# Transposing the logits' operand outside TensorE for 8 of 12 chunks of a fused attention and two-MoE kernel

## The chip, the cores and the metric

The kernel runs on one NeuronCore of a Trainium2 chip. The metric is the device time of one execution in microseconds (us), the median of several runs. Engines: PE is TensorE (PEld its weight loads), DVE is VectorE, ACT is ScalarE, POOL is GpSimd, SP is SyncE, whose queue issues every DMA of this kernel.

## The reference, cut to what matters

Block-causal attention is followed by a two-layer MLP and by a soft mixture of experts. Only the last one is touched: its `logits` need the tokens `x` with the model dimension on the partitions.

```python
# q, k, v: (8 batches, 8 heads, 576, 64), attention masked in blocks of 64
x = attn_out.transpose(0, 2, 1, 3).reshape(4608, 512)
h = np.maximum(x @ w_in, 0.0)             # 512 x 2048
x = h * h @ w_out                         # 2048 x 512
...
logits = x @ phi                          # 4608 x 512 by 512 x 32
d = np.exp(logits - logits.max(0)); d /= d.sum(0)
slot_input = d.T @ x                      # 32 slots x 512
slot_out = experts(slot_input)            # 8 experts, 4 slots each
c = np.exp(logits - logits.max(1)); c /= c.sum(1)
return c @ slot_out
```

## The kernel before, in words

The tokens are worked through in 12 chunks of 384 (three tiles of 128). A chunk of the MLP is 16 slots, one for each 128 columns of `w_in`. A slot has two parts on PE. `slot_h` (L808) makes 12 matmuls of 384 columns into the PSUM bank HB: the hidden layer of the slot, in three products, since weights and activations are each split in a high and a low part. ACT and DVE then make relu, square and the split (L814 to L819, tile MG). `slot_o` (L833) makes 9 matmuls of 512 columns into the three PSUM banks O, one for each token tile. The high parts of the weights (W) stay in SBUF; the low parts (WL) come back from DRAM for each slot, 512 KB, into one of three buffers (L800). A WL buffer is free when the sixth matmul of `slot_o`, three slots back, has read it, and it is needed by the second matmul of the slot's `slot_h`.

When a chunk's 16 slots are done, ACT (or DVE) copies the three O banks to X2 (L846, L847), and `moe2` does the soft mixture's part of the chunk beside the first slots of the next one. Before the change: 12 transposes on PE with the identity (L873), three copies from PSUM to the tile YA (L881, L882), the logits as 12 small matmuls that read YA (L888; each is two passes in the profile), a running maximum and sum, two more transposes (L917), and three matmuls of X2 (L940) that add to the slots' inputs. The attention of later batches (L447 scores, L456 to L493 softmax on DVE and ACT, L501 values) is spread over the slots too; it works in the SBUF tile aF and loads its keys and values through L433 and L434.

The order of the instructions on each engine is fixed when the program is built. `Program.order` plays the program through with costs per operation and gives each engine the ready operation of the earliest due time, so an operation that is expected later moves to a later place in the row, and the engine waits there if what it needs comes later still. Each engine works its row strictly in that order. SP too: a DMA that waits for data holds up every DMA behind it.

Of the kernel before, what the change touches and what calls it, by code (L numbers as in the profile page):

```python
# [7 lines left out]
F32 = mybir.dt.float32  # L8
# [7 lines left out]
NTOK, DM, DFF = B * S, H * D, 2048  # L16
NSLOT, NE, SPE, DFE = 32, 8, 4, 1024
KT = DM // 128
FT = DFF // 128
CH = 384  # L20
NCH = NTOK // CH
NTT = CH // 128
# [232 lines left out]
def c_tr(n):  # L255
    return 100 + 1.08 * n
# [6 lines left out]
def emit(tc, qk, v, vd, kq2, v2, w, phi, w1, w2, jsel, gsel, out):  # L263
    nc = tc.nc
    pe, act, dve, pool, sp = nc.tensor, nc.scalar, nc.vector, nc.gpsimd, nc.sync
    pr = Program()
# [8 lines left out]
    dram = tc.alloc_tile_pool(name="dram", bufs=1, space=bass.MemoryType.DRAM)  # L275
# [4 lines left out]
    BANKS = {"w": [psum.tile([128, 512], F32, name=f"B{t}") for t in range(4)], "w1": OB + [HB]}  # L280

    wlo_d = dram.tile([FT, 128, 1024], F32, name="wlo_d")
    part_d = dram.tile([NTT, 128, DM], F32, name="part_d")

    def bank(g):
        return BANKS[g.pool][g.bank]
# [5 lines left out]
    ph = cp.tile([128, KT, NSLOT], F32, name="ph")  # L292
# [4 lines left out]
    X2 = [cp.tile([128, DM], F32, name=f"X2_{i}") for i in range(NTT)]  # L297
    YA = cp.tile([128, NTT * DM], F32, name="YA")
# [20 lines left out]
    NPT = 2048  # L319
# [3 lines left out]
    L0, L1 = Lane(), Lane()  # L323
# [55 lines left out]
    def idle(keys):  # L379


        return [x for k in keys for x in list(pr.readers.get(k, ())) + ([pr.last_w[k]] if k in pr.last_w else [])]

    def parts(i):
        return range(2) if i == 4 else range(1)
# [4 lines left out]
    PT9, PH_ = 256, 2336  # L390
# [335 lines left out]
    YAK = [("YA", t) for t in range(NTT)]  # L726
# [132 lines left out]
    def moe2(c, m, due):  # L859

        z = m % 2
# [5 lines left out]
            return (nm, (z + o) % 2)  # L867

        xT = YA.rearrange("p (k n) -> p k n", k=KT)
        for t in range(NTT):  # L870
            g = Group("w")
            for k in range(KT):
                pr.add(("pe", c_mm(128), lambda g=g, t=t, k=k: pe.transpose(  # L873
                    bank(g)[:, k * 128:(k + 1) * 128], X2[t][:, k * 128:(k + 1) * 128], ident)),
                    r=[("X2", t), "id"], grp=g, take=(k == 0), due=due)
            d_ = xT[:, :, t * 128:(t + 1) * 128]

            def tb(g):
                return bank(g).rearrange("p (a b) -> p a b", a=KT)

            pr.add([("act", c_act(512), lambda g=g, d_=d_: act.copy(d_, tb(g))),  # L881
                    ("dve", c_tt(512), lambda g=g, d_=d_: dve.tensor_copy(d_, tb(g)))],  # L882
                   w=[("YA", t)], grp=g, give=True, due=due)
        g = Group("w")
        for k in range(KT):
            def mm(k=k, g=g):
                for t in range(NTT):
                    pe.matmul(bank(g)[32 * t:32 * t + 32, 0:128], ph[:, k], xT[:, k, t * 128:(t + 1) * 128],  # L888
                              start=(k == 0), stop=(k == KT - 1))
            pr.add(("pe", 206, mm), r=YAK + ["ph"], grp=g, take=(k == 0), due=due, mode=1)  # L890
        M, nM, sE = T("M"), T("nM"), T("sE")
        lg = g
        if m == 0:
            pr.add(("dve", c_tt(128), lambda: dve.reduce_max(M, bank(lg)[0:96, 0:128], axis=AX.X)),
                   w=[k2("M")], grp=g, due=due)
        else:
            mc = T("mc")
            pr.add(("dve", c_tt(128), lambda: dve.reduce_max(mc, bank(lg)[0:96, 0:128], axis=AX.X)),
                   w=[k2("mc")], grp=g, due=due)
# [8 lines left out]
        else:  # L908
            al = T("al")
            pr.add(("act", 188, lambda: act.activation(al, T("M", 1), AF.Exp, bias=nM)), r=[k2("M", 1), k2("nM")],  # L910
                   w=[k2("al")], due=due)
            pr.add(("dve", 70, lambda: dve.scalar_tensor_tensor(T("s"), T("s", 1), al, sE, ALU.mult, ALU.add)),
                   r=[k2("s", 1), k2("al"), k2("sE")], w=[k2("s")], due=due)
        g = Group("w")
# [123 lines left out]
    lR = [("a", nm, h) for h in range(2) for nm in ("hk", "hq", "ql", "kq")] + [("a", "v2")]  # L1038
    lF = [("a", "P2", i, h) for i in range(9) for h in range(2)] + [("a", "f", i) for i in range(5)]
    lF += [("a", "st"), ("a", "swap", 0), ("a", "swap", 1)] + [("a", nm, x) for nm in ("nm2", "sm2") for x in range(18)]  # L1040
    lF += [("a", "V"), ("a", "VD")] + [("a", "P", h, i, z_) for h in range(2) for i in range(5) for z_ in parts(i)]
    lF += [("a", "PT", x) for x in range(NPT // 64)] + [("a", nm, h) for h in range(2) for nm in ("rk", "rq")]
    xse = [("xs", c, k) for c in range(NCH - 3, NCH) for k in range(KT)]
# [399 lines left out]
```

## Time and profile before

| | |
|---|---|
| time, 3 runs | 1215.91 us median, 1214.48 to 1219.04 |
| the profiled execution | 1216.88 us, span of the profile 1215.1 us |
| PE busy | 1165.3 us of the span (96%) |
| DVE, ACT busy | 730.8 us (60%), 657.1 us (54%) |
| TensorE's granted clock, mean | 0.987 |
| DMA | 214.61 MB, 177 GB/s in the mean |

The times of instructions below are from the profiled execution; the rest of its own time, 1.8 us, lies around the span. A matmul's end in the profile is modelled and overlaps the next one, so what a group of matmuls costs is read from its first start to the start of what follows.

### The profile page before, as it was taken

To read this page: it belongs to the slowest core of one execution; us is meant where nothing else is said; L and a number is where in the kernel's file an instruction comes from. 1 tells how busy PE (TensorE), PEld (TensorE's weight loads), DVE (VectorE), ACT (ScalarE), POOL (GpSimd) and SP (SyncE) were. 2 spreads that over 40 slices of the span, in tenths; PEclk is the share of its full clock that TensorE was granted. 3 is DMA by queue.
4 is the path that set the end of the run, shared out by engine and by line. 5 is a ranking of instruction groups with operands and counts; after the bars stand their busy time and mean duration, and the time that the engine had idled before them with its cause. 6 is when DMAs were issued, how large, how long until landed. Compare 5 with 4: busy or idle time off the path is not lost.

```text
span 1215.1 us, 28105 instructions
## 1 busy us (share of the span) xinstructions
PE 1165.3 (96%) x11063; PEld 973.4 (80%) x11063; DVE 730.8 (60%) x2282; ACT 657.1 (54%) x2079; POOL 3.0 (0%) x16
## 2 busy tenths in 40 slices
PE   6887999999999999999999999999999999999994
PEld 5665887888888887888888888888888888989843
DVE  7999899957555556556557555566566552232213
ACT  7787697765545545545555554555554453242234
POOL 0000000000000000000000000000000000000000
PEclk9999999999999999999999999999999999999997
DMA  6598686543444443444443443443444337367898
GB/s 201 172 303 269 209 256 234 206 142 129 135 144 127 128 143 108 142 132 141 131 129 126 137 144 127 136 136 112 139 143 127 124 124 287 128 218 250 317 381 328
DMA packets 78468, 214.61 MB, mean 177 GB/s; under 512 B 14208, under 2 KB 26240, under 8 KB 78336
## 3 DMA queue, kind: packets, MB, share of 16 engines
q1 hardware_dynamic: 78336, 212.82, 52.2%
q8 instruction: 87, 1.43, 0.5%
q14 instruction: 45, 0.37, 0.1%
HBM read 194.17 MB, written 18.61 MB: 175 GB/s over the span
## 4 chain that ended last, share of the span: by engine, by line
PE 84%; DVE 8%; DMA 3%; ACT 2%; issue 1%; SPq 0%; ACTq 0%; DVEq 0%
PE HB L808 32%; PE O L833 31%; PE B L447 6%; PE B L501 5%; DVE anm L621 1%; DMA aF<-in_qk 1%; PE B L873 1%; PE B L888 1%; PE B L940 1%; PE O L1210 1%; PE B L598 1%; DVE aR L564 1%; DMA WL<-wlo_d 1%; DVE X L763 1%; PE B L1265 1%
## 5 line engine op out<-in xcount | busy, mean ns | idle before, releaser
L808 PE MATMUL HB<-MX,W 128*128 128x384 f32 x1536 | 441.4, 345 | 2.6 <-ACT R L814 1.7
L833 PE MATMUL O<-W,MG 128*128 128x512 f32 x1152 | 339.2, 398 | 1.1 <-DVE MG L817 1.0
L808 PEld LDWEIGHTS HB<-MX,W 128*128 128x128 f32 x1536 | 281.4, 189 | 18.0 <-issue 4.0
L808 PE MATMUL HB<-MX,WL 128*128 128x384 f32 x768 | 261.4, 340 | 0.8 <-DMA WL<-wlo_d 0.6
L833 PEld LDWEIGHTS O<-W,MG 128*128 128x128 f32 x1152 | 211.2, 188 | 38.8 <-issue 3.6
L463 ACT ACTIVATE aF<-B,aF 128x192 f32<-128x192 f32 (+8 forms) x432 | 166.9, 414 | 115.2 <-DVE aF L458 112.7
L817 DVE CAST MG<-R 128x384 fp32r<-128x384 f32 x149 | 53.2, 357 | 217.8 <-ACT R L815 215.5
L814 ACT ACTIVATE R<-HB 128x384 f32<-128x384 f32 x192 | 94.6, 493 | 153.9 <-PE HB L808 153.9
L833 PE MATMUL O<-WL,MG 128*128 128x512 f32 x576 | 167.4, 395 | 0.0
L456 DVE TENSOR_REDUCE aF<-B 128x1 f32<-128x192 f32 (+8 forms) x432 | 111.0, 316 | 79.4 <-PE B L447 79.1
L808 PEld LDWEIGHTS HB<-MX,WL 128*128 128x128 f32 x768 | 144.9, 189 | 10.0 <-DMA WL<-wlo_d 2.6
L833 PEld LDWEIGHTS O<-WL,MG 128*128 128x128 f32 x576 | 107.8, 188 | 25.7 <-issue 1.3
L819 DVE TENSOR_TENSOR MG<-R,MG 128x384 fp32r<-128x384 f32 x192 | 105.6, 550 | 8.6 <-ACT MG L817 0.5
L463 ACT ACTIVATION_READ_ACCUMULATOR aF<-B,aF 128x1 f32 x432 | 97.2, 225 | 0.0
L493 DVE STREAM_TRANSPOSE aF<-aF 128x256 f32<-128x256 f32 (+8 forms) x216 | 95.9, 486 | 0.5
L815 ACT ACTIVATE R<-R 128x384 f32<-128x384 f32 x147 | 77.3, 526 | 3.2
L447 PEld LDWEIGHTS B<-aR 64*32 64x32 f32 x3456 | 57.6, 105 | 22.2 <-issue 13.6
L447 PE MATMUL B<-aR 64*32 64x192 f32 (+8 forms) x3456 | 73.7, 301 | 0.0
L514 ACT COPY xr<-B 128x288 f32<-128x288 f32 x48 | 16.8, 403 | 100.0 <-PE B L501 100.0
L489 ACT ACTIVATE aF<-aF 128x256 f32<-128x256 f32 (+4 forms) x146 | 56.1, 435 | 26.1 <-DVE aF L483 26.1
L501 PEld LDWEIGHTS B<-aF,aR 64*64 64x64 f32 x1728 | 52.3, 133 | 18.7 <-issue 10.0
L501 PE MATMUL B<-aF,aR 64*64 64x192 f32 (+8 forms) x1728 | 66.4, 301 | 0.0
(257 smaller groups left out, 1193.6 us busy)
## 6 DMA issues: line engine op xcount, KB each, us to landing
WL<-wlo_d SPq DMA_DIRECT2D x187, 512.0 KB, 3.4
aR<-in_kq SPq DMA_DIRECT2D x24, 576.0 KB, 3.9
aR<-in_v SPq DMA_DIRECT2D x24, 576.0 KB, 3.7
Wr<-in_w SPq DMA_DIRECT2D x16, 512.0 KB, 4.8
aF<-in_w SPq DMA_DIRECT2D x13, 512.0 KB, 6.5
YA<-in_w SPq DMA_DIRECT2D x11, 512.0 KB, 4.4
call<-in_w SPq DMA_DIRECT2D x11, 512.0 KB, 3.8
wlo_d<-W SPq DMA_DIRECT2D x11, 512.0 KB, 5.3
```

The lines of the kernel that those rows point to most:

```text
L447: pe.matmul(bank(gs[h])[32 * g:32 * g + 32, c:c + 32 * i + 32].rearrange("p (b n) -> p b n", n=32), x[:, S + 64 * i + 32 * q_:S + 64 * i + ...
L456: pr.add(("dve", c_tt(n), lambda g=gs[h], n=n, c=c, x=x: dve.reduce_max(St[:, 0, x:x + 1], bank(g)[:, c:c + n], axis=AX.X, negate=True)), ...
L463: pr.add(("act", c_act(n, ext=2), lambda g=gs[h], n=n, c=c, x=x, i=i, h=h: act.activation(P_(i)[:, h], bank(g)[:, c:c + n], AF.Exp, bias=S ...
L489: act.activation(P_(i)[:, h], P_(i)[:, h], AF.Copy, scale=fct[:, x + h:x + h + 1])
L493: pr.add(("dve", c_tr(2 * n), lambda i=i: dve.transpose(P_(i), P_(i))), w=[K("P2", i, h) for h in range(2)])
L501: pe.matmul(bank(gs[q_])[64 * h:64 * h + 64, 32 * k:288].rearrange("p (i n) -> p i n", n=32), v_2()[sl, h, 64 * k:64 * k + 64], L0.F[sl, o ...
L808: pr.add(("pe", c_mm(CH), lambda a=a, b_=b_, sl=sl, n=n: pe.matmul(HB[:, 0:CH], (WL[i] if a == "l" else W[ft])[:, sl], b_, start=(n == 0), ...
L814: pr.add(("act", c_act(CH), lambda: act.activation(r_, HB[:, 0:CH], AF.Relu)), w=["HB", ("r", j)], due=-1)
L815: pr.add([("act", c_act(CH, True), lambda: act.activation(r_, r_, AF.Square)), ("dve", c_tt(CH), lambda: dve.tensor_mul(r_, r_, r_))], w=[ ...
L817: pr.add([("dve", c_cp(CH), lambda: dve.tensor_copy(gh, r_)), ("act", c_act(CH, True), lambda: act.copy(gh, r_))], r=[("r", j)], w=[("gh", ...
L819: pr.add(("dve", c_tt(CH), lambda: dve.tensor_sub(gl, r_, f(gh))), r=[("r", j), ("gh", j)], w=[("gl", j)], due=-1)
L833: pr.add(("pe", c_mm(512), lambda a=a, b_=b_, sl=sl, t=t, p_=p_: pe.matmul(OB[t], a[:, sl], (WL[i] if b_ == "l" else W[ft])[:, 512:1024], ...
```

## The change

For the chunks 2 to 9 (`blocks`), PE's transposes and their three copies go. DVE transposes each X2 tile in blocks of 32x32 into the tile XB (three instructions of 128x512), which lies in a part of aF. One DMA writes XB to DRAM (768 KB), and four DMAs of 192 KB read it back, one for each group of 32 partitions of YA, in pieces of 128 numbers (512 bytes), so that the blocks land on the partitions where the logits' matmuls want them. Those matmuls then read their moving operand in four runs of 32 columns. The chunks 0, 1, 10 and 11 stay as they were.

```diff
+    xt_d = dram.tile([2, NTT, 128, DM], F32, name="xt_d")
...
-        for t in range(NTT):
+        blocks = 2 <= m < NCH - 2
+        if blocks:
+            XB = L0.F[:, 2 * PH_:2 * PH_ + NTT * DM].rearrange("p (t n) -> p t n", t=NTT)
+            oldF = idle([("a", "PT", x) for x in range(NPT // 64)] + [("a", "V"), ("a", "VD")])
+
+            for t in range(NTT):
+                pr.add(("dve", c_tr(512), lambda t=t: dve.transpose(
+                    XB[:, t].rearrange("p (j k n) -> p j k n", j=4, k=KT), X2[t].rearrange("p (k j n) -> p j k n", k=KT, j=4))),
+                    r=[("X2", t)], w=[("a", "XB", t)], due=due, after=oldF)
+            pr.add(("sp", 50, lambda: sp.dma_start(xt_d[z].rearrange("t p n -> p t n"), XB)), r=[("a", "XB", t) for t in range(NTT)],
+                   w=[("xd", z)], due=due, nbytes=3 << 18)
+            for j in range(4):
+                pr.add(("sp", 50, lambda j=j: sp.dma_start(
+                    YA[32 * j:32 * j + 32].rearrange("p (g x) -> p g x", g=4 * NTT),
+                    xt_d[z].rearrange("t (g p) (j x) -> j p (t g) x", g=4, j=4)[j])), r=[("xd", z)],
+                    w=[("YA", t) for t in range(NTT)] if j == 0 else [("YAj", j)], due=due, nbytes=3 << 16)
+        for t in range(0 if blocks else NTT):
...
-                    pe.matmul(bank(g)[32 * t:32 * t + 32, 0:128], ph[:, k], xT[:, k, t * 128:(t + 1) * 128],
+                    x_ = xT[:, k, t * 128:(t + 1) * 128]
+                    if blocks:
+                        x_ = YA[:, t * DM:(t + 1) * DM].rearrange("p (g k n) -> p k g n", g=4, k=KT)[:, k]
+                    pe.matmul(bank(g)[32 * t:32 * t + 32, 0:128], ph[:, k], x_,
                               start=(k == 0), stop=(k == KT - 1))
```

The built program shows what moved. On PE, at the first slot after chunk 2 (rows of before, lines of before), the transposes stand between the matmuls of one `slot_h`:

```order
L808 MATMUL HB<-MX,W_81 128x384
L873 MATMUL B_72<-ident,X_0_89 128x128 x4
L873 MATMUL B_70<-ident,X_1_90 128x128 x4
L808 MATMUL HB<-MX,W_81 128x384
L808 MATMUL HB<-MX,WL_85 128x384
L808 MATMUL HB<-MX,W_81 128x384
L873 MATMUL B_72<-ident,X_2_91 128x128 x4
L808 MATMUL HB<-MX,W_81 128x384
```

The logits (L888) followed after the first matmul of the next `slot_o`. In the changed program, on PE, the transposes are gone from there, and the logits (now L910) stand two slots later: after three whole parts `slot_h` and two whole parts `slot_o`, behind the second matmul of the third `slot_o` (here L834, one line down; the last row of the third `slot_h`, L809, is the first row shown).

```order
L809 MATMUL HB<-MX,W_84 128x384
L834 MATMUL O_65<-W_83,MG 128x512
L834 MATMUL O_66<-W_83,MG 128x512
L910 MATMUL B_70<-YA,ph 32x128 x12
L834 MATMUL O_67<-W_83,MG 128x512
L834 MATMUL O_65<-WL_87,MG 128x512
```

So three whole `slot_h` and two whole `slot_o` stand between the chunk's end and the logits, where one `slot_h` with the transposes and one matmul stood. On SP, at the same place in the changed program, between the loads of keys, values and WL (L434, L435, L801), the write of XB (L882) and the four loads of YA (L885) come in, with one WL load between them and the next WL load behind them:

```order
L434 DMA aR_2068<-in_kq 128x1152
L801 DMA WL_87<-wlo_d 128x1024
L882 DMA xt_d<-aF 128x3x512
L801 DMA WL_85<-wlo_d 128x1024
L885 DMA YA<-xt_d 32x12x128 x4
L801 DMA WL_86<-wlo_d 128x1024
```

Before, the WL loads stood one behind the other there. On DVE, at the same place in the changed program, the three transposes (L879) stand right behind the attention's row maxima (L457) and ahead of the next split of the hidden layer (L818, L820):

```order
L457 TENSOR_REDUCE aF<-B_71 128x1
L879 STREAM_TRANSPOSE aF<-X_0_90 128x512
L879 STREAM_TRANSPOSE aF<-X_1_91 128x512
L879 STREAM_TRANSPOSE aF<-X_2_92 128x512
L459 TENSOR_SCALAR aF<-aF 128x8
L818 CAST MG<-R_96 128x384
L820 TENSOR_TENSOR MG<-R_96,MG 128x384
```

Before, DVE had nothing of `moe2` there until the logits' maximum; the three copies to YA were ACT's.

## Rows read from the trace of the kernel before

**Rows 1.** The page, busy time by engine and the span.

```profile
span 1215.1 us, 28105 instructions
PE 1165.3 (96%) x11063; PEld 973.4 (80%) x11063; DVE 730.8 (60%) x2282; ACT 657.1 (54%) x2079; POOL 3.0 (0%) x16
```

**Rows 2.** The page, the chain that ended last, shares by line.

```profile
PE HB L808 32%; PE O L833 31%; PE B L447 6%; PE B L501 5%; DVE anm L621 1%; DMA aF<-in_qk 1%; PE B L873 1%; PE B L888 1%; PE B L940 1%; PE O L1210 1%; PE B L598 1%; DVE aR L564 1%; DMA WL<-wlo_d 1%; DVE X L763 1%; PE B L1265 1%
```

**Rows 3.** One line's instructions, L873: duration ns min/median/max, first and last start.

```profile
L873 PE MATMUL B<-ident,X x144: 270/272/330, 252.0 to 1144.6; 128*128 128x128 f32 x144
```

**Rows 4.** PE's timeline after chunk 2: start us, us.

```profile
385.14 0.33 PE L808 MATMUL HB<-MX,W 128*128 128x384 f32 x1
...
385.66 1.03 PE L873 MATMUL B<-ident,X 128*128 128x128 f32 x8
386.45 0.42 PE L808 MATMUL HB<-MX,W 128*128 128x384 f32 x1
...
388.57 0.40 PE L833 MATMUL O<-W,MG 128*128 128x512 f32 x1
388.89 1.07 PE L888 MATMUL B<-YA,ph 128*32 128x128 f32 x24
```

**Rows 5.** What PE waited for ahead of L888: us, times.

```profile
  ACT YA L881: 2.7, 8
  DVE YA L882: 0.7, 2
  issue: 0.6, 3
```

**Rows 6.** PE's timeline, a slot with no other work in it.

```profile
397.63 0.33 PE L808 MATMUL HB<-MX,W 128*128 128x384 f32 x1
...
399.74 0.86 PE L833 MATMUL O<-W,MG 128*128 128x512 f32 x3
...
401.82 0.34 PE L808 MATMUL HB<-MX,W 128*128 128x384 f32 x1
402.00 0.34 PE L808 MATMUL HB<-MX,WL 128*128 128x384 f32 x1
```

**Rows 7.** Groups of instructions by shape: busy us, mean ns | idle before.

```profile
L493 DVE STREAM_TRANSPOSE aF<-aF 128x512 f32<-128x512 f32 x24 | 16.1, 671 | 0.0
...
L888 PE MATMUL B<-YA,ph 128*32 128x128 f32 x288 | 13.6, 276 | 0.1
...
L501 PE MATMUL B<-aF,aR 64*64 64x128 f32 x192 | 9.6, 269 | 0.0
```

**Rows 8.** ACT's timeline after chunk 2.

```profile
384.88 1.56 ACT L846 COPY X<-O 128x512 f32<-128x512 f32 x3
```

**Rows 9.** DVE's timeline after chunk 2.

```profile
385.16 0.45 DVE L456 TENSOR_REDUCE aF<-B 128x1 f32<-128x96 f32 x3
```

**Rows 10.** DMA issues: KB each, median us from issue to landing.

```profile
WL<-wlo_d SPq DMA_DIRECT2D x187, 512.0 KB, 3.4
...
wlo_d<-W SPq DMA_DIRECT2D x11, 512.0 KB, 5.3
...
wlo_d<-WL SPq DMA_DIRECT2D x5, 512.0 KB, 3.2
...
out<-Wr SPq DMA_DIRECT2D x6, 256.0 KB, 2.8
...
aF<-in_qk SPq DMA_DIRECT2D x4, 192.0 KB, 3.7
...
YA<-part_d SPq DMA_DIRECT2D x1, 768.0 KB, 4.6
...
aF<-in_qk SPq DMA_DIRECT2D x4, 128.0 KB, 6.0
```

**Rows 11.** Who waited for the WL loads (us, times), and their landing.

```profile
  PEld HB L808: 2.6, 6
  PE HB L808: 0.6, 2
...
DMA to landing us min/median/max: 3.0/3.4/8.3
```

**Rows 12.** SP's timeline: an undisturbed WL load; loads behind chunk 9.

```profile
397.13 0.32 SPq L800 DMA_DIRECT2D WL<-wlo_d  x1
...
1000.91 2.59 SPq L1127 DMA_DIRECT2D aF<-in_w  x5
```

More of the change, by code (lines that the diff above doesn't have):

```diff
@@ L887, in mm @@
                 for t in range(NTT):
-                    pe.matmul(bank(g)[32 * t:32 * t + 32, 0:128], ph[:, k], xT[:, k, t * 128:(t + 1) * 128],
+                    x_ = xT[:, k, t * 128:(t + 1) * 128]
+                    if blocks:
+                        x_ = YA[:, t * DM:(t + 1) * DM].rearrange("p (g k n) -> p k g n", g=4, k=KT)[:, k]
+                    pe.matmul(bank(g)[32 * t:32 * t + 32, 0:128], ph[:, k], x_,
                               start=(k == 0), stop=(k == KT - 1))
-            pr.add(("pe", 206, mm), r=YAK + ["ph"], grp=g, take=(k == 0), due=due, mode=1)
+            pr.add(("pe", 206, mm), r=YAK + ["ph"] + ([("YAj", j) for j in range(1, 4)] if blocks else []), grp=g, take=(k == 0), due=due, mode=1)
         M, nM, sE = T("M"), T("nM"), T("sE")
@@ L1040, in emit @@
     lF += [("a", "st"), ("a", "swap", 0), ("a", "swap", 1)] + [("a", nm, x) for nm in ("nm2", "sm2") for x in range(18)]
+    lF += [("a", "XB", t) for t in range(NTT)]
     lF += [("a", "V"), ("a", "VD")] + [("a", "P", h, i, z_) for h in range(2) for i in range(5) for z_ in parts(i)]
```

## The prediction

> **What bounds the kernel now.** I read the page's busy times first: PE is busy 1165.3 us of a span of 1215.1 us, DVE 60% and ACT 54% [rows 1]. Then the chain that ended last: two thirds of it are the MLP's matmuls at L808 and L833, and the other PE lines, among them L873 and L888 with 1% each, follow [rows 2]. The third view is PE's timeline in a stretch where a slot has no other work: `slot_h` begins at 397.63, `slot_o` at 399.74, the next `slot_h` at 401.82 [rows 6]. That is 2.11 and 2.08 us without a gap, so in the stretch of the change the end moves with every matmul that PE gets rid of, and with every wait that PE gets. What the reader is to see: the order on PE is fixed, so nothing else fills a wait there. The question is whether what is taken off PE is more than the waits that come in.
>
> **What the change removes.** The 144 transposes of before are 12 a chunk [rows 3]; 96 of them go. Their price is read from the slot behind chunk 2. Its `slot_h` runs from 385.14 to 388.57, 3.43 us [rows 4], where an undisturbed one takes 2.11 [rows 6]: **1.32 us** a chunk. The eight at 385.66 took 0.79 us up to the next start, 0.099 each, so 1.19 for twelve; the other 0.13 is lost where the stream of matmuls is broken. Eight chunks: **10.6 us**. Ahead of the logits PE waited for the copies to YA: 2.7, 0.7 and 0.6 us [rows 5], 4.0 over twelve chunks, 0.33 each.
>
> **What it adds, in order of time, at chunk 2.** I set the chunk's end at 385.14, where the next `slot_h` begins.
> ACT's three copies to X2 are done at 384.88 + 1.56 = 386.44 [rows 8]. DVE is through with the row maxima ahead of the transposes at 385.61 [rows 9]. A transpose of 128x512 on DVE took 671 ns in the attention [rows 7], so three end 2.01 us later, at 387.6, none having to wait for its copy. The split of the hidden layer, which stands behind them on DVE, needs ACT's relu and square of a `slot_h` that ends at 387.25, and so comes later than 387.6 by itself: the transposes are covered there. If DVE has attention work ahead of them (as at the ends of chunks 4 and 7), all that follows moves by as much.
> The store of 768 KB is issued at about 387.7. No store of this size stands alone in the trace. 256 KB took 2.8 us and 512 KB 3.2 in quiet stretches, 512 KB 5.3 in the crowded first part [rows 10]. Two steps of 0.4 per 256 KB give **3.6 us**, and that is what I take, since beside this store only a WL load runs; the bounds are 2.8 and 5.3 + 0.4 = 5.7. It lands at 391.3.
> The four loads wait for that on SP, and each issue takes 0.32 us [rows 12], so the last goes out 1.0 us behind the first. A load of 192 KB took 3.7 us, so the four are there after 4.7 at the least. The only loads in pieces of 512 bytes (128 KB of keys in the crowded start) took 6.0, which gives 7.0 as the upper bound. One load of 768 KB took 4.6 [rows 10]. I take **4.7**: these queues are quiet here. The operand is complete at 396.0.
> PE comes to the logits after three `slot_h`, two `slot_o` and two matmuls: 385.14 + 3 x 2.11 + 2 x 2.08 + 2 x 0.23 = 396.1. So operand and PE meet within 0.1 us. As the order puts the logits at the margin in the old program too, where 0.33 us were lost, I take the same 0.33 for the new wait: old and new cancel. At the bounds the operand comes 0.8 us sooner (no wait at all) or 2.1 + 2.3 = 4.4 us later.
> The logits themselves: no row has this shape with a moving operand in runs of 32. L501 reads its operand in such runs, and 128 columns of it took 269 ns against 276 of L888, which reads in one run [rows 7]. I price it at nothing.
>
> [...]
>
> **WL loads.** An undisturbed one is issued at 397.13 and used at 402.00 [rows 6, 12]; it lands after 3.4 us [rows 11], so it has 1.5 us to spare. The first WL load behind the store is issued when the sixth matmul of the next `slot_o` is through, 388.6 to 388.9, some 1.2 us behind the store. What 768 KB ahead cost it lies between 1.2 us (0.4 per 256 KB, the quiet stores) and 3.6 us (512 to 768 KB, 3.4 to 4.6, the loads), less the 1.2 of lead: 0 to 2.4 us, against 1.5 to spare. The second is issued behind the four loads, but the logits (1.0 us, from L888's 13.6 us over twelve chunks) run before its use, so it has 2.5. I take 0.1 us of waiting a chunk, **0.8 us**; if the cover is gone, it is up to 0.9 a chunk.
>
> **Chunk 9.** The expert weights that go into aF, five loads of 512 KB in 2.59 us at 1000.91 [rows 12], now have to wait until XB has been written, and stand seven in a row between two WL loads. At 0.4 us per 256 KB that is 5.6 us in front of a WL load which has 1.5 to spare, and the logits, the slots' sums and a reordered `slot_o` lie in between. I take **1.2 us** once, between 0 and 4.
>
> **Sum.** Against the profiled execution's own time: 1216.88 - 10.6 + 0.8 + 1.2 = 1208.3. The median of the runs shown is 1.0 below that execution, so **1207.3**.
>
> **The rivals.**
> *The round trip eats the gain.* Operand late by about 1 us more than taken: 8 x 1.0 = 8 us, **1215**. For it: the margin is 0.1 us, and each of store, loads and DVE's queue is a step with a spread of that size. Against: the values taken come from quiet rows, and the stretch moves little data.
> *The round trip is much slower, and the kernel gets slower.* The place is PE's wait ahead of the logits; it decides from 8.6 / 8 = 1.1 us of lateness on, and from 1.8 on the loss can be measured. At both upper bounds, 4.4 us late, the time is 1207.3 + 35 = **1242**; with the loads alone at their bound, 2.3 late, 1207.3 + 18 = **1226**. For it: small pieces and few partitions, which no quiet row shows. Against: the rows of the upper bounds are from the crowded start. [...]
> *SP's queue is the price.* The two WL loads a chunk come late by 0.7 us each: 11 us, **1218**. For it: 3.2 us of PE waits for WL are there already [rows 11]. Against: 1.5 and 2.5 us to spare.
> *No wait at all.* Everything lands early, and the old waits go too: 8 x 0.33 = 2.7 and the two terms of 2.0 fall away: **1202.6**.
> That the transposes filled time which PE would have lost anyway is not borne out, since the slot around them is 1.32 us longer than one without.
>
> **How the numbers follow.** About 0.5% (6.1 us) is what a measurement of this kernel can tell from no change. The forecast, 1203 to 1210, has 0.50; no wait at all 0.05; the eaten gain 0.21; SP's queue 0.08; the slower round trip 0.16. Up to 1203 lie 0.05, and over 1221 some 0.13, from the slower round trip: the range is 1203 to 1221. Faster than 1209.8 is the forecast nearly whole and the case of no wait, 0.54; slower than 1222 is the slower round trip, less its weak end, and a little of SP's queue, 0.16; 0.30 remain.
>
> **What would show it.** In the profile after: L873 with 48 matmuls in place of 144; undisturbed `slot_h` parts of 2.11 us behind the chunks 2 to 9; the three transposes at 0.67 us; the store's landing near 3.6 and the loads' near 3.7 to 4.7 us; PE's wait ahead of the logits near 0.33 us a chunk; waits for WL of 4 to 5 us in all. The prediction is wrong if the wait for YA's loads exceeds 1.1 us a chunk, if WL waits go over 8 us, or if DVE, now with 24 more transposes, holds up `slot_o` through the tile MG.

## The result, and the profile after

The changed kernel took 1231.78 us (median of 6 runs, 1226.84 to 1235.96), the kernel before 1216.35 us beside it (6 runs): a ratio of 1.011, 95% interval 1.010 to 1.013. It is slower by 1.1%, where 0.7% faster was forecast, and the time lies 10.8 us above the range. The profiled execution took 1234.42 us.

The page after, span and busy times, then the chain that ended last (compare [rows 1, 2]; all line numbers of the changed kernel are shifted, L808 is L809, L833 is L834, L888 is L910):

```profile
span 1232.6 us, 27961 instructions
PE 1161.8 (94%) x10967; PEld 967.9 (79%) x10967; DVE 736.1 (60%) x2289; ACT 654.7 (53%) x2072; POOL 3.0 (0%) x16
...
PE HB L809 28%; PE O L834 28%; PE B L448 6%; PE B L502 5%; DMA YA<-xt_d 3%; DMA xt_d<-aF 3%; DMA WL<-wlo_d 2%; PE B L910 1%; DMA wlo_d<-W 1%; DVE anm L622 1%; PE O L1233 1%; PE B L962 1%; SPq L885 1%; DVE aF L879 1%; DMA aF<-in_qk 1%
```

PE is busy 3.5 us less and the span is 17.5 us longer. Two transfers that the chain did not have, the store and the loads, now hold 3% of it each.

Groups of instructions by shape, after (busy us, mean ns of one | idle before them):

```profile
L910 PE MATMUL B<-YA,ph 128*32 128x128 f32 x288 | 16.2, 321 | 17.2 <-DMA YA<-xt_d 15.2 <-ACT aF L464 2.0
L892 PE MATMUL B<-ident,X 128*128 128x128 f32 x48 | 7.0, 276 | 0.0
```

The transposes are down to 48, as the change says. PE now stands idle 17.2 us ahead of the logits, where it was 0.1 us [rows 7] (the 2.0 put down to ACT are chunk 3's wait for its loads too: the last landed at 488.50, and the logits began at 488.70), and a logits' matmul takes 321 ns in the mean where it took 276. Both are seen at chunk 2. PE's timeline there, after:

```profile
384.17 0.33 PE L809 MATMUL HB<-MX,W 128*128 128x384 f32 x1
...
386.27 0.86 PE L834 MATMUL O<-W,MG 128*128 128x512 f32 x3
...
392.73 0.33 PE L809 MATMUL HB<-MX,W 128*128 128x384 f32 x1
...
394.84 0.63 PE L834 MATMUL O<-W,MG 128*128 128x512 f32 x2
398.90 1.80 PE L910 MATMUL B<-YA,ph 128*32 128x128 f32 x24 [3.44 <-DMA YA<-xt_d]
400.64 0.80 PE L834 MATMUL O<-W,MG 128*128 128x512 f32 x1
401.23 1.44 PE L834 MATMUL O<-WL,MG 128*128 128x512 f32 x3
402.51 0.86 PE L834 MATMUL O<-W,MG 128*128 128x512 f32 x3
```

Chunk 2's end, counted as in the prediction from the start of the `slot_h` that held the transposes, is now at 384.17. That `slot_h` takes 2.10 us (to 386.27) in place of 3.43 [rows 4], and the third one 2.11 (392.73 to 394.84), so the gain of the removed transposes is there. Then PE waits 3.44 us. Behind the wait three matmuls are busy for 1.44 us (401.23), the next three for 0.86 (402.51): for 3.4 us the granted clock was half. The windows of the five such stretches, behind chunks 2, 4, 6, 7 and 9 (us, busy us of each engine and instructions, PEclk, DMA share, GB/s):

```profile
399.10:402.50 3.40, 3.40 (x28) 2.64 (x23) 1.75 (x7) 0.82 (x4) 0.00 (x0) 0.50 0.00 1
580.00:583.40 3.40, 3.35 (x56) 2.38 (x64) 0.59 (x3) 0.86 (x4) 0.00 (x0) 0.50 0.01 4
757.50:760.90 3.40, 3.01 (x28) 2.49 (x29) 0.59 (x3) 0.70 (x4) 0.00 (x0) 0.50 0.32 128
849.60:853.00 3.40, 3.38 (x61) 2.40 (x69) 0.59 (x3) 0.90 (x4) 0.00 (x0) 0.51 0.06 20
1040.80:1047.60 6.80, 6.22 (x20) 5.52 (x19) 0.92 (x2) 1.61 (x4) 0.00 (x0) 0.50 0.27 112
```

That is 20.4 us at a granted clock of 0.50 to 0.51. PE was busy for 19.4 of them; half of that, 9.7 us, is my estimate of what the clock cost. The kernel before has a granted clock of 1.00 over the whole of 300 to 1050 us. Four of the stretches follow waits for the loads of 2.3 to 3.4 us; behind those of 0.6 to 2.0 us (chunks 3, 5, 8 and 9) the clock stayed at 1.00. The fifth has another cause. PE's timeline behind chunk 9, after, and SP's:

```profile
1036.78 0.85 PE L834 MATMUL O<-W,MG 128*128 128x512 f32 x3
1039.39 0.44 PE L809 MATMUL HB<-MX,WL 128*128 128x384 f32 x1 [1.75 <-DMA WL<-wlo_d]
```

```profile
1023.50 4.23 SPq L1150 DMA_DIRECT2D aF<-in_w  x7
1029.13 0.33 SPq L801 DMA_DIRECT2D WL<-wlo_d  x1
```

Seven loads of expert weights, 512 KB each, now go out at once when XB has been written to DRAM (five before, [rows 12]); the WL load behind them took 10.2 us to land, and PE waited 1.75 us for it.

SP's timeline at chunk 2, after, and the summary of the four loads' line L885 (who waited: us, times):

```profile
386.46 0.37 SPq L882 DMA_DIRECT2D xt_d<-aF  x1
387.85 0.32 SPq L801 DMA_DIRECT2D WL<-wlo_d  x1
390.29 1.87 SPq L885 DMA_DIRECT2D YA<-xt_d  x4
392.26 1.16 SPq L801 DMA_DIRECT2D WL<-wlo_d  x1
```

```profile
L885 SPq DMA_DIRECT2D YA<-xt_d x32: 318/467/1507, 390.3 to 1022.1; - x32
...
  PE B L910: 15.2, 7
  PEld B L910: 6.6, 2
...
DMA to landing us min/median/max: 2.7/4.8/7.1
```

The store (L882) was issued at 386.46 and the loads that wait for it went out at 390.29, so it took 3.8 us. From the first load's issue to the logits are 8.6 us. Over the eight chunks the records of issue and landing give 3.4 to 5.8 us for the store, mean 4.5, and 8.5, 6.9, 7.2, 7.0, 8.0, 6.4, 7.4 and 6.3 us from the first issue to the last landing, mean 7.2. Each load takes 4.8 us in the median from its own issue, but the four land one behind the other, 1.09 us apart in the mean. PE's matmuls waited 4.1 us for WL loads (L801), against 0.6 before [rows 11]; 1.9 of it lie ahead of chunk 2's end, where none of the new transfers runs (why that part differs from kernel to kernel is open), and 1.75 are chunk 9's.

### The profile page after: what moved, and what is told of

It reads as the page before. It is cut to its first block, busy times and chain, and to the rows that moved or that the text cites. A ratio compares the mean times of both kernels' runs of the same rounds, so it can differ in the third digit from the quotient of the medians.

```text
span 1232.6 us, 27961 instructions
## 1 busy us (share of the span) xinstructions
PE 1161.8 (94%) x10967; PEld 967.9 (79%) x10967; DVE 736.1 (60%) x2289; ACT 654.7 (53%) x2072; POOL 3.0 (0%) x16
## 4 chain that ended last, share of the span: by engine, by line
PE 75%; DMA 10%; DVE 9%; ACT 3%; issue 1%; SPq 1%; ACTq 0%; DVEq 0%
PE HB L809 28%; PE O L834 28%; PE B L448 6%; PE B L502 5%; DMA YA<-xt_d 3%; DMA xt_d<-aF 3%; DMA WL<-wlo_d 2%; PE B L910 1%; DMA wlo_d<-W 1%; DVE anm L622 1%; PE O L1233 1%; PE B L962 1%; SPq L885 1%; DVE aF L879 1%; DMA aF<-in_qk 1%
## 5 line engine op out<-in xcount | busy, mean ns | idle before, releaser
L809 PE MATMUL HB<-MX,W 128*128 128x384 f32 x1536 | 440.2, 346 | 3.9 <-ACT R L815 2.6
L834 PE MATMUL O<-W,MG 128*128 128x512 f32 x1152 | 339.7, 399 | 1.1 <-DVE MG L818 1.0
L809 PEld LDWEIGHTS HB<-MX,W 128*128 128x128 f32 x1536 | 282.8, 190 | 19.4 <-ACT R L815 5.0
L809 PE MATMUL HB<-MX,WL 128*128 128x384 f32 x768 | 263.2, 343 | 4.1 <-DMA WL<-wlo_d 4.1
L834 PEld LDWEIGHTS O<-W,MG 128*128 128x128 f32 x1152 | 212.0, 188 | 40.1 <-issue 4.5
L818 DVE CAST MG<-R 128x384 fp32r<-128x384 f32 x146 | 52.0, 356 | 207.8 <-ACT R L816 206.2
L834 PE MATMUL O<-WL,MG 128*128 128x512 f32 x576 | 167.7, 396 | 0.0
L457 DVE TENSOR_REDUCE aF<-B 128x1 f32<-128x192 f32 (+8 forms) x432 | 111.4, 314 | 84.7 <-PE B L448 84.4
L809 PEld LDWEIGHTS HB<-MX,WL 128*128 128x128 f32 x768 | 145.8, 190 | 14.5 <-DMA WL<-wlo_d 7.4
L834 PEld LDWEIGHTS O<-WL,MG 128*128 128x128 f32 x576 | 108.1, 189 | 27.4 <-issue 3.0
L820 DVE TENSOR_TENSOR MG<-R,MG 128x384 fp32r<-128x384 f32 x192 | 105.5, 549 | 10.4 <-ACT MG L818 2.2
L816 ACT ACTIVATE R<-R 128x384 f32<-128x384 f32 x152 | 79.9, 526 | 3.2
L448 PEld LDWEIGHTS B<-aR 64*32 64x32 f32 x3456 | 57.7, 107 | 22.8 <-issue 14.2
L490 ACT ACTIVATE aF<-aF 128x256 f32<-128x256 f32 (+4 forms) x146 | 55.6, 435 | 23.2 <-DVE aF L484 23.2
```

What stands on the lines that cost most here:

```text
L448: pe.matmul(bank(gs[h])[32 * g:32 * g + 32, c:c + 32 * i + 32].rearrange("p (b n) -> p b n", n=32), x[:, S + 64 * i + 32 * q_:S + 64 * i + ...
L457: pr.add(("dve", c_tt(n), lambda g=gs[h], n=n, c=c, x=x: dve.reduce_max(St[:, 0, x:x + 1], bank(g)[:, c:c + n], axis=AX.X, negate=True)), ...
L490: act.activation(P_(i)[:, h], P_(i)[:, h], AF.Copy, scale=fct[:, x + h:x + h + 1])
L809: pr.add(("pe", c_mm(CH), lambda a=a, b_=b_, sl=sl, n=n: pe.matmul(HB[:, 0:CH], (WL[i] if a == "l" else W[ft])[:, sl], b_, start=(n == 0), ...
L816: pr.add([("act", c_act(CH, True), lambda: act.activation(r_, r_, AF.Square)), ("dve", c_tt(CH), lambda: dve.tensor_mul(r_, r_, r_))], w=[ ...
L818: pr.add([("dve", c_cp(CH), lambda: dve.tensor_copy(gh, r_)), ("act", c_act(CH, True), lambda: act.copy(gh, r_))], r=[("r", j)], w=[("gh", ...
```

## The experiments

**The theory:** the gain is real; the four loads, each to 32 partitions, follow each other too slowly, so the operand comes 2 to 4 us behind PE, and the half clock follows from these waits. **The rivals:** the pieces of 512 bytes make the loads slow; WL loads delayed on SP's queue are the price; the gain isn't real.

All runs in one table. "Idle" is PE's idle time ahead of the logits, "WL" PE's wait for WL loads (matmul rows; the prediction and the expectations add the weight loads' rows, which overlap with these: 3.2 before, 11.5 in the changed kernel), "loads" the mean from the first load's issue to the last landing, all us in the profiled execution. Ratios are to the kernel before on the same chip.

```
run                 median   ratio [95%]             span    idle  WL   loads
before              1216-19                          1215.1   0.1  0.6   -
after               1231.8   1.011 [1.010, 1.013]    1232.6  17.2  4.1  7.2
e1_told             1214.6   0.996 [0.994, 0.997]    1212.8   0.1  4.5  6.9
e2_direct           1208.7   0.992 [0.989, 0.994]    1204.4   0.0  0.6   -
e3_all_partitions   1220.9   one run                 1219.1   6.9  4.3  8.8
e4_long_rows        1233.2   one run                 1231.4  14.2  5.3  6.9
e5_wide             1283.8   1.054 [1.052, 1.055]    1282.3  61.2  1.2   -
e6_wide_told        1271.0   1.043 [1.042, 1.045]    1268.4  45.9  0.9   -
e7_filled           1241.5   1.019 [1.016, 1.021]    1241.4   4.7  3.5  7.2
e8_traffic          1223.9   1.004 [1.002, 1.005]    1225.5   0.1  6.3   -
e9_even             1217.0   0.999 [0.998, 1.001]    1213.2   6.8  3.4  5.8
e10_even_told       1213.7   0.996 [0.994, 0.997]    1211.3   0.6  6.0  5.6
e11_one             1211.8   0.994 [0.993, 0.996]    1210.0   2.2  3.1  5.5
e12_halves          1213.3   0.996 [0.994, 0.997]    1213.6   1.5  5.7   -
```

**e1_told: the logits later.** One number of the planner:

```diff
-  w=[("YA", t) ...] if j == 0 else [("YAj", j)], due=due, nbytes=3 << 16)
+  w=[("YA", t) ...] if j == 0 else [("YAj", j)], due=due, nbytes=8 << 16)
```

> The changed kernel with one number of the planner different: each of the four loads to YA is told to be 8/3 as long, so that the logits of chunks 2 to 9 are put further back in PE's row and nothing else is added or taken away. Theory (the four loads land one behind the other about 1 us apart, so the operand is 2 to 4 us late for the place where the logits stand, and the half clock behind those waits comes from them): PE's waits ahead of the logits fall from about 18 us to under 4 us in all, the stretches at half clock behind chunks 2 to 9 go, and the time falls by 14 to 24 us against the changed kernel, to 1207 to 1217 us. Rival (SP's queue: the WL loads issued behind the four loads are late, whatever the place of the logits): the waits for the logits go, but PE's waits for WL rise above the 11.5 us that they are in the changed kernel, and the time stays at or above 1220 us. Second rival (taking the transposes off PE gains nothing in truth): 1217 us or more with neither kind of wait in the profile.

The loads are hardly faster (6.9 us), but the logits come 1.8 to 2.8 us behind the last landing in six chunks of eight. Its groups by shape:

```profile
L910 PE MATMUL B<-YA,ph 128*32 128x128 f32 x288 | 12.9, 276 | 0.1
```

The idle time goes, the matmuls are back at 276 ns, the clock stays full behind chunks 2 to 9 (1.00 in the mean of 300 to 1050 us), and the time falls by 17 us to 0.4% under the kernel before. The wait, with the clock behind it, was the price; WL's share hardly changes (4.5 us, 2.5 of them ahead of chunk 2's end). Both rivals of this run fall.

**e2_direct: the gain by itself.** Store and loads out, the logits' operand read from XB:

```diff
-  x_ = YA[:, t * DM:(t + 1) * DM].rearrange("p (g k n) -> p k g n", g=4, k=KT)[:, k]
+  x_ = XB[:, t].rearrange("p (g k n) -> p k g n", g=4, k=KT)[:, k]
```

> The way through DRAM is left out: no store, no loads, and the logits of chunks 2 to 9 read XB as VectorE wrote it, so their operand's rows are not in the order that the reference needs; everything else is computed as before. It measures what taking the transposes off PE is worth by itself. Theory (the gain of 1.32 us a chunk is real, and all that the changed kernel loses is lost in the way through DRAM): 1202 to 1208 us, no wait ahead of the logits above 0.5 us a chunk, WL waits near the 3.2 us of before, granted clock full behind chunks 2 to 9. Rival (the gain isn't there, or reading the moving operand in runs of 32 costs it): 1212 to 1218 us, with the logits' matmuls longer than 0.28 us each.

Its groups by shape, the eight chunks and the other four:

```profile
L903 PE MATMUL B<-aF,ph 128*32 128x128 f32 x192 | 8.6, 276 | 0.0
L903 PE MATMUL B<-YA,ph 128*32 128x128 f32 x96 | 4.3, 276 | 0.0
```

The span is 10.7 us under that of before; the forecast's term was 10.6. From chunk 2's end to the end of the last `slot_o`, where the change lies, e2 takes 748.0 us and the kernel before 758.1, 10.1 us more. The median is 9.9 us under that of the kernel before on the same chip, and 0.7 us above the expected range. Reading in runs of 32 costs nothing: 276 and 276 ns.

**e3_all_partitions and e4_long_rows: partitions or pieces.**

```diff
 e3:
-  for j in range(4): ... YA[32 * j:32 * j + 32] ...
+  for t in range(NTT): ... YA.rearrange("p (j t x) -> p t j x", t=NTT, j=4)[:, t], xt_d[z, t].rearrange("p (j x) -> p j x", j=4)
 e4:
-  xt_d[z].rearrange("t (g p) (j x) -> j p (t g) x", g=4, j=4)[j]
+  xt_d[z].rearrange("t p n -> (t p n)").rearrange("(j p g x) -> j p g x", j=4, p=32, g=4 * NTT)[j]
```

> The four loads to 32 partitions each are replaced by three loads to all 128 partitions, one per token tile, of the same 768 KB in pieces of the same 512 bytes; the exchange between partition groups is left out, so the logits read rows in a wrong order. Theory (what makes the loads slow is that each reaches only 32 partitions): the last of the loads lands 4 to 5 us behind the first issue, in place of 6.3 to 8.5 us, landings 0.4 to 0.6 us apart, waits ahead of the logits under 6 us in all, time 1210 to 1220 us. Rival (the pieces of 512 bytes make them slow): the last lands 6 to 8 us behind the first issue as in the changed kernel, and the time stays at 1226 to 1236 us.

> The four loads go to 32 partitions each as in the changed kernel, but each partition takes 6 KB in one run of DRAM in place of twelve pieces of 512 bytes; the rearrangement is left out, so the logits read wrong rows. Theory (32 partitions make the loads slow): landings still about 1 us apart, the last 6 to 8 us behind the first issue, waits ahead of the logits about 18 us in all, time 1226 to 1236 us. Rival (the pieces make them slow): the last lands within 5 us of the first issue, waits under 6 us in all, 1210 to 1220 us.

e4 is clear: with 6 KB in one run the loads still land 0.95 us apart (1.09 with the pieces), PE stands idle 14.2 us and the time does not move. So the pieces are at most a small part. e3 did not come out as a clean test. SP's timeline at chunk 2:

```profile
392.97 0.56 SPq L885 DMA_DIRECT2D YA<-xt_d  x1
394.96 0.33 SPq L801 DMA_DIRECT2D WL<-wlo_d  x1
395.34 1.30 SPq L885 DMA_DIRECT2D YA<-xt_d  x2
```

My edit made the planner hold the second load back behind the first, so a WL load with its own wait came between, and the time from first issue to last landing grew to 8.8 us. The second and third load, issued together, landed 0.74 us apart for 256 KB each; per byte that is half of a step in the changed kernel. It speaks for the partitions, but the kernel's time, 0.9 us over the theory's range, says nothing.

**e5_wide and e6_wide_told: all partitions, whole computation.** The copy in DRAM laid out as [partition][column block][tile], and each load going to all 128 partitions; e6 has `6 << 16` besides:

```diff
-  YA[32 * j:32 * j + 32]..., xt_d[z].rearrange("t (g p) (j x) -> j p (t g) x", g=4, j=4)[j]
+  YA[:, 384 * j:384 * j + 384], xt_d[z].rearrange("(g p) (j x) -> g j p x", g=4, j=4)[j]
```

> The changed kernel with another layout of the copy in DRAM: XB keeps the block column ahead of the token tile, the store writes one run of 6 KB per partition, and each of the four loads goes to all 128 partitions (pieces of 1.5 KB) in place of 32. Same 768 KB each way, same order on every queue and engine; the whole computation is done. Theory (each load to 32 partitions takes about 1.05 us behind the one before it, and that makes the operand late): landings 0.5 to 0.7 us apart, the last 4.5 to 5.5 us behind the first issue in place of 6.3 to 8.5, PE's waits ahead of the logits 2 to 7 us in all in place of 18, WL waits under 9 us, time 1208 to 1216 us. Rival (the round trip through DRAM is slow in whatever form, by latency or by other traffic): last landing still over 6 us, time over 1222 us.

> As the kernel with loads to all partitions, and the planner told that each load is twice as long, so that the logits stand further back in PE's row. Theory: waits ahead of the logits under 1 us in all, WL waits 3 to 8 us, time 1205 to 1212 us, which is faster than the kernel before by 0.4 to 1.0%. Rival (what is left of the loss is in the DMA traffic or in SP's queue, not in the wait): no more than 0.3% from the kernel before, 1213 to 1220 us, with WL waits over 10 us.

The theory fails in both: 5.4% and 4.3% slower. e5's time is the one of its rival (over 1222 us), but for another reason than the rival's; e6 fits neither. e5's DMA from 393.4 to 405.2 us in 40 slices, the busy tenths of the 16 engines and the rate:

```profile
DMA  8952330002222229425999962222222222222222
GB/s 347 361 236 111 52 36 31 0 26 83 99 83 94 104 89 252 113 113 196 363 413 271 224 146 76 104 94 99 99 104 94 104 94 104 104 102 87 113 111 111
```

For whole stretches the queue moves about 100 GB/s, a quarter of the 394 to 417 of e11 below. From 401.5 to 405.2 us, at 102 GB/s, the 16 DMA engines were busy for 0.27 of the time, so some four of them at once (an estimate from that share). Each of e5's loads reads DRAM with the four column blocks outermost. e9 below changes that order and nothing else in the loads: its loads moved, with one WL load behind them as here, 238 GB/s in the mean of 390.3 to 397.2 us, where the view above has a mean of 136. It was a slip of mine, not a test of the theory.

**e9_even, e10_even_told, e11_one: all partitions, done properly.** The column block goes innermost in the partition number, so that each load of e9 and e10 reads one run of DRAM:

```diff
+  ph4: rows of ph in the order 4p + j, loaded by
+  sp.dma_start(ph4.rearrange("q k n -> q (k n)"), phi.rearrange("(j p) k n -> p j (k n)", j=4))
 e9, e10 (e10: nbytes=5 << 16):
+  YA[:, 384 * j:384 * j + 384], xt_d[z].rearrange("(g p) (j x) -> g (p j) x", g=4, j=4)[j]
 e11, one load (nbytes=4 << 18):
+  YA.rearrange("q (g x) -> q g x", g=4), xt_d[z].rearrange("(g p) (j x) -> (p j) g x", g=4, j=4)
```

> The earlier kernel with loads to all partitions moved 100 GB/s and kept only 4 transfers going at a time by its trace, because each load's source had the four column blocks as its outer dimension; so it did not test the 32 partitions. Here the four loads again go to all 128 partitions in pieces of 1.5 KB, but the block column is put in the innermost place of the partition number (partition 4p+j in place of 32j+p), so that each load reads 192 KB of DRAM in one run; the logits' other operand gets its rows in the same order through a second small load at the start. The whole computation is done, and the order on queues and engines is that of the changed kernel. Theory (the 32 partitions per load make the operand late): landings 0.4 to 0.7 us apart, the last 4.3 to 5.5 us behind the first issue, PE's waits ahead of the logits 1 to 7 us in all, time 1208 to 1217 us. Rival (DRAM round trip slow in any form): last landing over 6 us behind the first issue, time over 1222 us.

> The same, and the planner told 5/3 of each load's length, so that the logits stand later in PE's row. Theory: waits ahead of the logits under 1 us in all, WL waits 4 to 9 us, 1206 to 1212 us, faster than the kernel before by 0.4 to 1.0%. Rival (traffic and SP's queue are what is left): 1213 to 1219 us with WL waits over 10 us.

> The same layout with one load of 768 KB in place of four, the planner told 4/3 of its length. Theory (what counts is how many partitions and transfers are at work at once, not the number of loads): landing 4.2 to 5.2 us behind the issue, SP's queue free 1.1 us sooner for the WL loads, waits ahead of the logits under 2 us in all, 1205 to 1211 us. Rival (four loads land sooner since they spread over more of the queue): landing over 6 us, 1215 us or more.

e9 differs from the changed kernel in the layout alone (128 partitions to a load, pieces of 1.5 KB); the order on PE and SP is the same but for the one small load of ph4 at the start. e4 has that order too, and its loads, like e9's, each read 192 KB of DRAM in one run; so between these two the partitions differ, and the pieces, which are longer in e4. Its groups by shape:

```profile
L910 PE MATMUL B<-YA,ph 128*32 128x128 f32 x288 | 12.9, 275 | 6.8 <-DMA YA<-xt_d 5.7 <-ACT aF L465 1.1
```

The loads are there after 5.8 us in place of 7.2, idle time falls from 17.2 to 6.8, and the time by 14.7 us, to that of the kernel before. The landings are mostly 0.5 us apart, which is how fast the loads are issued, but in five chunks of eight one or two come 1.1 to 1.9 us behind the one ahead, so that the 5.8 stay above the expected 5.5; why is open. Behind its longest wait, 1.94 us at chunk 7, the granted clock was half once more, for 3.4 us. e11's rate while its load runs, from 477.2 to 482.5 us:

```profile
GB/s 0 0 0 0 62 216 309 93 124 124 216 309 309 464 402 433 309 244 410 421 383 371 406 394 406 417 394 394 406 394 406 417 325 255 290 402 139 174 243 278
```

and the changed kernel's while its four run, from 390.25 to 398.75 us:

```profile
GB/s 328 347 347 405 231 162 171 193 272 229 292 279 193 152 140 149 301 282 275 222 224 263 181 186 229 239 263 231 207 166 222 200 142 161 137 58 58 19 19 19
```

400 GB/s against 140 to 300, and a long tail. The DMA engines were busy for 0.82 of the changed kernel's window and 0.87 of e11's, so it was not for want of engines at work. e10 and e11 put the logits a little later too and are faster than the kernel before by 0.4% and 0.6%: the best versions found, although both missed their expected ranges, e11 (1205 to 1211) by 0.8 us, e10 (1206 to 1212) by 1.7. e10 came out by its rival's numbers (1213 to 1219, waits for WL over 10 us, by both rows 14.8); of the 6.0 us of matmul waits 2.9 lie ahead of chunk 2's end and 2.5 are chunk 9's.

**e7_filled: what the half clock does.** In the closure of the changed kernel's logits, for k = 0, 24 matmuls on XB first:

```diff
+  for n in range(8 * NTT if blocks and k == 0 else 0):
+      a, b_ = n % NTT, n // NTT % KT
+      pe.matmul(bank(g)[32 * a:32 * a + 32, 0:128], ph[:, b_], XB[:, a]...[:, b_], start=True, stop=True)
```

> The changed kernel with 24 idle matmuls on XB in front of each chunk's logits (two sets of the size of the logits, about 2.0 us a chunk, in the bank that the logits then overwrite), so that PE works through most of the wait for the loads; nothing is left out. Theory (the granted clock falls to half because PE stands still, and that costs about 10 us of the 17 over the kernel before): the stretches at half clock behind chunks 2 to 9 go, the waits shrink to under 5 us, and the time falls by 6 to 12 us to 1219 to 1226 us though the logits come no sooner. Rival (the half clock lies beside other work or would come anyway): 1228 to 1236 us, no change.

The time went up, and both numbers miss: chunk 9's filling had to wait 8.4 us for the expert weights that go into the same tile, and the filling takes about 1.8 us a chunk even where the wait is shorter. So the size of the clock's share is not settled by it. Its windows show where the clock fell and where it stayed: behind chunk 4, where 3.4 us of wait were left, behind chunk 9, and over chunks 2 and 3, where the filling left none:

```profile
580.60:587.40 6.80, 5.72 (x78) 4.30 (x79) 2.30 (x10) 1.72 (x7) 0.00 (x0) 0.50 0.03 10
1031.20:1041.40 10.20, 5.68 (x73) 4.79 (x74) 0.28 (x1) 0.00 (x0) 0.00 (x0) 0.50 0.45 161
386.00:560.00 174.00, 173.87 (x1919) 148.94 (x1918) 103.62 (x331) 89.62 (x332) 0.00 (x0) 1.00 0.48 153
```

Where PE was kept at work the clock stayed at 1.00, though the loads took as long as before (7.2 us in the mean). So it did at chunks 6 and 7, where waits of 0.4 and 1.0 us were left; behind these and chunk 2 it had fallen in the changed kernel.

**e8_traffic and e12_halves: what the traffic costs.** e8 is the kernel before with VectorE's transposes, the store and the loads added, the loads into a part of aF that nobody reads; e12 is e11 with two loads of 384 KB, the second put behind a WL load:

```diff
 e8:
-  YA[32 * j:32 * j + 32].rearrange("p (g x) -> p g x", g=4 * NTT)
+  L0.F[:, 6208:6208 + NTT * DM][32 * j:32 * j + 32].rearrange("p (g x) -> p g x", g=4 * NTT)
 e12:
+  w=YAK + [("YAj", 1)] if j == 0 else [("YAj", 1)], due=due, nbytes=5 << 17
```

> The kernel before with the change's work on VectorE and the queues alone: the logits of all twelve chunks take their operand from TensorE's transposes as before, while for chunks 2 to 9 VectorE also transposes X2 into XB, and the store and the four loads run into a part of aF that nobody reads. Nothing of the computation is left out. Theory (beside the wait for the operand the traffic costs little: WL loads delayed behind the loads): WL waits 6 to 12 us in place of 3.2, time 1218 to 1223 us, so 2 to 6 us over the kernel before. Rival (SP's queue and contention are the main price): 1226 us or more.

> The layout with even loads once more, now two loads of 384 KB; the planner is made to put the second behind the end of the first, so that a WL load goes between them, and is told 5/3 of their length, so that the logits stand further back. It asks what the 6 us are that still lie between the best kernel so far and the one that leaves out the way through DRAM. Theory (WL loads stuck behind 768 KB of loads): PE's waits for WL fall from 10 to 15 us in all to under 6 us, no waits ahead of the logits, 1206 to 1210 us, 0.7 to 1.1% faster than the kernel before. Rival (the WL loads are late because the transfers share the DMA engines, in whatever order): WL waits still over 9 us, 1211 to 1215 us.

Who waited for WL loads, e8 (us, times):

```profile
  PEld HB L809: 8.7, 6
  PE HB L809: 6.3, 5
```

and e12:

```profile
  PEld HB L810: 8.7, 8
  PE HB L810: 5.7, 7
```

In e8 the traffic alone makes the kernel 0.2 to 0.5% slower, 5 us, which is 0.9 us over the theory's 1223 and below the rival's 1226; its waits for WL, 15.0 us by both rows, pass the theory's 12. From chunk 2's end to the end of the last `slot_o` it takes 761.6 us, 3.5 more than the kernel before. Of its 6.3 us of matmul waits 3.9 lie ahead of chunk 2's end, 2.0 are chunk 9's wait behind the expert weights, and 0.4 is all the rest. In e12 a WL load goes ahead of the second half, and the waits for WL do not fall (behind chunk 2's end 2.2 us, against e11's 1.6; the other 3.5 lie ahead of it), and the time does not beat e11's: the theory that WL loads stand behind 768 KB falls, by the rival's numbers. The rival's own reason, shared DMA engines, is only argued. From chunk 2's end to the end of the last `slot_o` e2 takes 748.0 us, e11 753.0, e10 754.5 and e12 756.1. Waits for WL and for the operand make 3.7 to 3.8 us of these 5.0 to 8.1. In e10 the clock was half for 3.4 us besides, at its wait of 2.5 us for chunk 9's WL; the rest I could not place.

## Why the prediction was wrong

**The gain: right.** 10.6 us were forecast and 10.7 measured in e2, 10.1 of them in the stretch of the change. The undisturbed `slot_h` is 2.11 us, the three transposes on VectorE take 671 ns each in the median and hold up no split (the waits for MG stay at 1.0 us), though they are part of the way to the store, and the moving operand in runs of 32 costs nothing (276 ns a matmul in e2 with and without).

**The store: nearly.** 3.6 us were taken, the mean was 4.5, between 3.4 and 5.8; at chunk 2, counted from the chunk's end (384.17 in place of 385.14), it was issued 0.3 us sooner than worked out and landed 0.1 sooner.

**The loads: the step that failed.** "I take 4.7: these queues are quiet here." They took 7.2 us in the mean, just over the upper bound of 7.0. PE reached the logits of chunk 2 at 395.3 (394.84 and two matmuls of 0.23), 11.1 us behind the chunk's end where I had 11.0, and the operand came at 398.77, 14.6 us behind it where I had 10.9: the loads took 8.5 us there. The margin of 0.1 us made every tenth of this a wait. If each group of loads had landed 4.7 us behind its first issue, and all else stayed, 1.1 us of the 17.2 would be left, at chunks 4 and 7, whose stores took 5.8 us (an estimate from the issues and waits of the eight chunks). The 4.7 was read from rows of loads to all partitions [rows 10], and no row had 32. The queues' traffic is the smaller part at most: e9 and e11, in the same stretch and with the same neighbours, get the same bytes in 5.8 and 5.5. So 1.4 to 1.7 of the 2.5 us went with the partitions; 0.8 to 1.1 over the 4.7 stay, and why is open. e4 shows that it isn't the 512 bytes: its loads, 6 KB in one run, still land 0.95 us apart, against 1.09 in the changed kernel and the 0.32 between two issues that I had counted on. Small pieces and few partitions had only a part of a chance of 0.16.

**The old wait against the new one: failed with it.** They were to cancel at 0.33 us a chunk; the new one is 17.2 us in all, 2.1 a chunk, over the 1.1 that was to show the prediction wrong.

**The half clock: no term at all.** I had priced a wait at its own length. After four of the eight waits and behind chunk 9's wait for WL the granted clock was half for 20.4 us, 9.7 us by the estimate from PE's busy time in them; before, that stretch had none. The account of the 29.1 us between e2 (748.0) and the changed kernel (777.1), from chunk 2's end to the end of the last `slot_o`: 17.2 idle ahead of the logits, 2.2 of waiting for WL, and the 9.7 worked out for the clock, 29.1 in all. A run that changes the clock alone is missing, since e7 failed as one. But in e1, where 17.2 us of these waits go and the clock stays full, the same stretch gets 23.2 us shorter (753.9), about 6 us more than the waits.

**WL loads: right in size. Chunk 9: too small.** Ordinary WL waits behind chunk 2 are 0.4 us (0.8 taken): the rival of SP's queue is excluded by e1. Counted as in the prediction, over both rows and the whole span, the waits are 11.5 us, past its sign of 8; the matmuls' part of them is 4.1, and 1.9 of that lie ahead of the first new transfer. Chunk 9 was to cost 1.2, at most 4; its 1.75 us wait, 0.6 us more right behind it and 6.8 us of half clock make up to 5.7 us. The place was right, the clock was missing here too.

**The rivals.** What came is "the round trip is much slower", between its 1226 (loads at their bound) and its 1242 (both at theirs). Its place was right, PE's wait ahead of the logits; its chance was not, and the range should have reached into it. That the time lies within its bounds is luck in part: by its price, which is the wait alone, the waits measured give 1207.3 - 2.7 + 17.2 = 1221.8, hardly past the range, and the rest is the half clock, which no rival had.

## What to carry to other kernels

Price a way through DRAM from rows of the same partitions, or measure it, and count to the last landing of the group and not to one: here the last of four loads to 32 partitions each landed 7.2 us behind the first issue, and the same bytes to 128 partitions took 5.5 to 5.8 us. Where it meets a consumer that has no slack, tell whatever orders the work the true length first: one number was worth 17 us here, the better layout alone 15. And a wait cost more than its own length here: behind those of 2.3 to 3.4 us at chunks 2, 4, 6 and 7 the granted clock was 0.50 to 0.51 for 3.4 us, which is 1.5 to 1.7 us more each by half of PE's busy time (an estimate).

## What I had not expected of the hardware

That the granted clock fell to half behind single waits of 1.75 to 3.4 us, in an execution otherwise 94% busy, though not behind others of up to 2.0 us (1.94 us brought it down in e9, 1.96 did not in the changed kernel), and that it stayed up where idle matmuls filled the wait (e7, chunk 2). And what the order of dimensions on one side of a load was worth: e5's four loads to all 128 partitions moved about 100 GB/s for whole stretches and 136 in the mean of 393.4 to 405.2 us, e9's, in the other order, 238 in the mean of 390.3 to 397.2, and e11's one load of the same 768 KB 400.
